# Linear attention and a gated linear unit on one core: output stored by one transfer a chunk instead of four, a head pair of q loaded by two instead of four

## The chip, the cores and the metric

The kernel runs on one core of a Trainium2 chip. The core has a matrix engine (TensorE, PE in the profile, with PEld for its weight loads), VectorE (DVE), ScalarE (ACT), GpSimd (POOL) and SyncE (SP), which computes nothing and issues transfers. Sixteen DMA engines move data between HBM and the core's memory, whichever queue issues the transfer. The metric is device time in microseconds of one execution.

## The reference

Two blocks follow each other. The first is linear attention with a norm for each head, the second a gated linear unit whose gate is a causal convolution over five tokens. There are 8 batches, 8 heads, 576 tokens, a head dimension of 64 (so 512 channels), all in float32; the weights arrive in float64.

```python
kv = einsum('bhsd,bhse->bhde', k, v)
out = einsum('bhsd,bhde->bhse', q, kv)
rms = sqrt(mean(out * out, axis=-1, keepdims=True) + 1e-06)
x = (out / rms * g_norm)            # then (B, H, S, D) -> (B, S, H*D)
gate = sigmoid(sum over k of conv_w[k] * x shifted by K-1-k tokens)
result = (gate * (x @ w_val)) @ w_out
```

## The kernel before

The whole order of the work is written out by hand in a list of some 1,200 steps (PLAN); each step is a function with its arguments, called in the list's order, and each engine and each queue runs its instructions in that order. Waits between them follow from the tiles that they read and write. Work of neighbouring batches is interleaved: while TensorE multiplies batch b by the weights, q, k and v of batches b + 1 and b + 2 are loaded, and the output of a pair of batches is stored later.

For a batch b the steps are:

- load_half (lines 302 to 311) loads half of k or v, 576 KB, in one transfer of 128 rows of two runs of 2,304 B. The k and v tiles of batches 2 to 7 have one buffer for each half, so the next load waits for kv_product.
- load_q (313 to 325) loads one pair of heads of q for batches 2 to 7. Batches 0 and 1 use load_q_rows (327) instead. Tokens stand in memory as token = t x 18 + n, with t from 0 to 31 and n from 0 to 17; a row t is one run of 18 x 64 values. The tile qs has room for three loads, so a load waits until the load three earlier has been transposed. It holds, for each of two heads r and for each half of the head dimension, 32 partitions t; the second half is read 32 values (128 B) further on, and each partition takes 1,120 values (4,480 B).
- turn_q (460) transposes 32 x 32 blocks on VectorE. Then kv_product (432) and raw_pair and raw_tail (via raw_product, 488) multiply on TensorE; square, sums, powers and normalise scale by the root.
- turn_blocks (595) transposes x on VectorE, and move_blocks (599) carries the blocks to their place by transfers within the core's memory, alternately on SP's and GpSimd's queue.
- gate_start, gate_tap, gate_end form the gate, val_fast (669) multiplies by w_val, gated multiplies the two.
- For a pair of batches i, fast_product (755) and out_product (707) multiply by w_out, and fast_keep (778) and keep_out (726) collect a chunk c of 128 rows in the tile ot, which has three buffers. Chunks 0 to 3 and 4 to 7 are the first 512 tokens of the two batches; chunk 8 holds the last 64 tokens of both.
- store (802) writes a chunk. The 128 partitions of ot are four blocks j of 32 tokens t; the output is viewed as rows_out[batch, n, t, channel], in which neighbouring t lie 18 x 512 values apart and neighbouring n 512 values. The last two chunks are stored by store_last (799), in two halves, one on SP's queue and one on ACT's.

All loads of q for batches 2 to 7 and nearly all stores go through SP's queue. SP takes eight completion counters in turn; a transfer waits until the one eight before it has landed.

Of the kernel before, what the change touches and what calls it, by code (L numbers as in the profile page):

```python
# [207 lines left out]
def kernel(  # L208
# [11 lines left out]
    nc = tc.nc  # L220
    B, H, S, D = q.shape
    C = H * D
    HP = H // 2
    NJ = S // P
    SF = NJ * P
    T = S - SF
    NK = C // P
    TB = 32
    NB = S // TB
# [3 lines left out]
    HB = P // TB  # L233
# [62 lines left out]
    st = {}  # L296

    def head(hp, r):

        return r * (H // 2) + hp  # L300
# [12 lines left out]
    def load_q(b, hp):  # L313
        t = qs[:, (b * HP + hp + 1) % 3]
        run = S // TB * D - TB
        flat = t.rearrange("p n d -> p (n d)")
        for half in range(2):
            for r in range(2):
                first = (2 * r + half) * TB
                nc.sync.dma_start(  # L320
                    out=flat[first:first + TB, 0:run],
                    in_=q[b, head(hp, r)].rearrange("(t n) d -> t (n d)", t=TB)[
                        :, half * TB:half * TB + run],
                )
        st["q", b, hp] = t

    def load_q_rows(b, r):
# [377 lines left out]
    rows_out = out.rearrange("b (t n) c -> b n t c", n=NB)  # L705
# [93 lines left out]
    def store_last(i, c, n):  # L799
        store(i, c, nc.scalar if n else nc.sync, range(n * HB // 2, (n + 1) * HB // 2))  # L800

    def store(i, c, queue=nc.sync, blocks=range(HB)):
        ot = st["ot", i, c]
        for j in blocks:
            bb, n = divmod(c * HB + j, NJ * HB) if c < 2 * NJ else (j // 2, NJ * HB + j % 2)
            queue.dma_start(out=rows_out[2 * i + bb, n], in_=ot[j * TB:(j + 1) * TB, :])

    steps = {f.__name__: f for f in (
        load_half, load_q, load_q_rows, stage_weight, narrow_weight, turn_cw, keep_cw, start_warm, warm_up,
        kv_product, kv_copy, turn_q, turn_q_rows, sort_q, raw_whole, raw_pair, raw_tail, square, sums, powers, normalise,  # L810
        turn_x, keep_x, turn_blocks, move_blocks, halo, gate_start, gate_tap, gate_end, val_product, keep_val, gated,
        val_sums, x_sums, val_fast, val_keep, out_product, keep_out, weight_sums, token_sums, fast_product, fast_keep,
        store, store_last)}
    with tc.manual_schedule():
        set_up()
# [33 lines left out]
```

## Time and profile before

| what | value |
|---|---|
| median of three runs | 306.25 us (304.12 to 307.25) |
| span of the profiled execution | 304.6 us |
| transfers issued by SP | 325 |
| HBM read, written | 39.21 MB, 9.44 MB |
| issue of one q load or one store on SP, median | 0.42 us each |
| transpose of one q tile on VectorE (two instructions) | 0.70 and 0.20 us |

All times below are from one profiled execution, whose span is 304.6 us; the runs' median is 1.65 us above it. In the profile a line such as L320 is a line of the kernel, SPq is SP's queue, and a group's row gives how many instructions it has, their busy time and the mean of one. The views in forty columns cut the span in equal slices of 7.6 us, each digit a tenth of busy time. The rows of the issue table give the size of one transfer and the median time from its issue to its landing. Of the kernel's time TensorE's matrix products are the largest part: the product with w_out (L774), with w_val (L682 and L633) and the attention products (L440, L501).

### The profile page before, as it was taken

The page shows a single profiled execution, that of the slowest core. Times are in us where ns is not written, and L with a number is a line of the kernel's source. Part 1 is how long each engine was busy: PE and PEld are TensorE (multiplying, and loading weights), DVE is VectorE, ACT ScalarE, POOL GpSimd, SP SyncE. Part 2 cuts the span into 40 slices and gives each one's busy share as a digit, 9 for nine tenths or more (in the row PEclk, how much of TensorE's full clock was granted, in tenths as well). Part 3 has the DMA queues.
Part 4 walks back from the last instruction along what each step waited for, and adds up shares of the span by engine and source line. Part 5 has one row for each costly group of instructions (what it writes and reads, how often), then busy time and mean ns, then how long its engine had stood idle before and what let it go on. Part 6 is the DMA issues. An engine that isn't in the chain of part 4 may idle for free.

```text
span 304.6 us, 8977 instructions
## 1 busy us (share of the span) xinstructions
PE 294.8 (97%) x3441; PEld 232.4 (76%) x3441; DVE 269.2 (88%) x474; ACT 193.7 (64%) x596; POOL 114.9 (38%) x127
## 2 busy tenths in 40 slices
PE   7899999999999999999999999999999999999993
PEld 7788778877787785777778757787878588888582
DVE  1169999999999999999999999999999999999612
ACT  1569989999768664884586547683787354535220
POOL 3027354406568217364338352345536631000000
PEclk9979999999999999999999999999999999999999
DMA  7999998088569756988689477927411621112423
GB/s 269 343 368 343 272 302 210 4 230 269 154 147 329 231 163 167 269 220 260 173 253 294 111 175 232 326 72 214 114 48 30 169 80 34 36 42 64 103 69 103
DMA packets 32074, 55.53 MB, mean 182 GB/s; under 512 B 6166, under 2 KB 14358, under 8 KB 32032
## 3 DMA queue, kind: packets, MB, share of 16 engines
q1 hardware_dynamic: 29520, 49.76, 55.7%
q0 software_dynamic: 1632, 3.17, 4.1%
q10 hardware_dynamic: 880, 2.03, 1.8%
q8 instruction: 27, 0.44, 0.6%
q14 instruction: 15, 0.12, 0.1%
HBM read 39.21 MB, written 9.44 MB: 160 GB/s over the span
## 4 chain that ended last, share of the span: by engine, by line
PE 89%; DVE 5%; DMA 2%; issue 1%; ACT 1%; DVEq 0%; ACTq 0%; SPq 0%
PE a L774 18%; PE cb L774 14%; PE va L682 13%; PE val L633 11%; PE vc L682 6%; PE kvps L440 6%; PE raw L501 5%; PE out L720 5%; PE vb L682 4%; PE qTps L477 4%; PE raw L512 2%; PE xTps L583 2%; DMA qs<-in_q_dram 2%; DVE gate L621 2%; DVE xs L667 1%
## 5 line engine op out<-in xcount | busy, mean ns | idle before, releaser
L552 POOL TENSOR_TENSOR rt<-ss,mhalf 128x8 f32<-128x8 f32 (+3 forms) x38 | 68.9, 1822 | 101.0 <-DVE ss L544 100.8
L621 DVE SCALAR_TENSOR_TENSOR gate<-xT,cwT,gate 128x576 f32<-128x576 f32 x128 | 101.8, 809 | 1.0
L571 ACT ACTIVATE x<-raw,rt 128x64 f32<-128x64 f32 x252 | 55.8, 351 | 7.2 <-POOL rt L552 4.2
L604 POOL DMA_DIRECT2D xT<-y x48 | 26.4, 557 | 25.5 <-DVE ot L784 14.0
L633 PE MATMUL val<-xT,wval 128*128 128x288 f32 x128 | 33.0, 411 | 0.0
L774 PE MATMUL a<-wsum,sums 128*128 128x256 f32 x128 | 32.4, 382 | 0.0
L628 ACT ACTIVATE gate<-gate 128x576 f32<-128x576 f32 x32 | 22.0, 692 | 11.7 <-DVE gate L621 11.4
L633 PEld LDWEIGHTS val<-xT,wval 128*128 128x128 f32 x128 | 23.5, 190 | 6.5 <-ACT xT L590 0.4
L544 DVE TENSOR_REDUCE ss<-sq 128x8 f32<-128x520 f32 (+1 forms) x40 | 24.7, 627 | 2.9 <-ACT sq L531 2.5
L774 PEld LDWEIGHTS a<-wsum,sums 128*128 128x128 f32 x128 | 24.0, 190 | 4.1 <-issue 0.6
L535 ACT ACTIVATE sq<-raw 128x256 f32<-128x256 f32 (+1 forms) x70 | 22.4, 403 | 7.3 <-PE raw L501 7.1
L682 PE MATMUL va<-xs,vsum 128*128 128x288 f32 x96 | 26.6, 409 | 0.0
L615 ACT ACTIVATE gate<-xT,cwT 128x576 f32<-128x576 f32 x32 | 25.2, 811 | 1.5 <-DVE gv L646 1.3
L646 DVE TENSOR_TENSOR gv<-gv,gate 128x576 f32<-128x576 f32 x32 | 23.6, 750 | 0.9 <-ACT gate L628 0.8
L682 PEld LDWEIGHTS va<-xs,vsum 128*128 128x128 f32 x96 | 18.0, 190 | 5.1 <-ACT x L571 0.4
L611 POOL COPY xT<-xT 128x124 f32<-128x124 f32 x32 | 17.5, 585 | 10.5 <-ACT xT L590 10.5
L501 PEld LDWEIGHTS raw<-kv,qT 64*64 64x64 f32 x1008 | 16.4, 134 | 5.3 <-issue 3.0
L440 PEld LDWEIGHTS kvps<-v,k 64*64 64x64 f32 x1008 | 15.9, 135 | 3.7 <-issue 1.9
L501 PE MATMUL raw<-kv,qT 64*64 64x64 f32 x1008 | 18.7, 221 | 0.0
L440 PE MATMUL kvps<-v,k 64*64 64x64 f32 x1008 | 17.6, 220 | 0.0
L774 PE MATMUL cb<-wsum,sums 128*128 128x256 f32 x64 | 16.9, 386 | 0.1
L774 PE MATMUL cb<-wout,gv 128*128 128x256 f32 x64 | 16.8, 385 | 0.0
(111 smaller groups left out, 542.3 us busy)
## 6 DMA issues: line engine op xcount, KB each, us to landing
qs<-in_q_dram SPq DMA_DIRECT2D x96, 140.0 KB, 4.2
out_dram<-ot SPq DMA_DIRECT2D x140, 64.0 KB, 1.7
k<-in_k_dram SPq DMA_DIRECT2D x14, 576.0 KB, 6.3
v<-in_v_dram SPq DMA_DIRECT2D x12, 576.0 KB, 6.5
xT<-y SPq DMA_DIRECT2D x48, 64.0 KB, 2.7
xT<-y POOLq DMA_DIRECT2D x48, 64.0 KB, 3.3
y<-in_moe_w_val_dram SPq DMA_DIRECT2D x4, 512.0 KB, 11.4
w_wout<-in_moe_w_out_dram SPq DMA_DIRECT2D x4, 512.0 KB, 6.3
```

What stands on the lines that cost most here:

```text
L440: nc.tensor.matmul(st["kvps", b][s][r * D:(r + 1) * D, i], st["k", b, i][rows, r, cols], st["v", b, i][rows, r, cols], start=(j == 0), sto ...
L501: nc.tensor.matmul(st["raw", b, c][r][cols, to * D:(to + 1) * D], st["qT", b][rows, hp, first:first + D], kvs[b % 2][rows, hp, :], start=T ...
L544: nc.vector.reduce_sum(out=st["ss", b][:, FIRST[c]:FIRST[c] + n], in_=st["sq", b, c][:, 0:n], axis=AX.X)
L552: nc.gpsimd.tensor_tensor(out=st["rt", b][:, which], in0=st["ss", b][:, which], in1=mhalf[:, which], op=ALU.pow)
L571: nc.scalar.activation(out=x[:, to * D:(to + 1) * D], in_=raw[:, h * D:(h + 1) * D], func=AF.Copy, scale=root[:, to:to + 1])
L604: (nc.sync if i % 2 else nc.gpsimd).dma_start(out=xTs[b % 2][i * TB:(i + 1) * TB, :, first:first + P], in_=y[a * TB:(a + 1) * TB, i])
L615: nc.scalar.activation(out=gate[:], in_=xTs[b % 2][:, jt, HALO:SX], func=AF.Copy, scale=cwT[:, K - 1, jt:jt + 1])
L621: nc.vector.scalar_tensor_tensor(out=gate[:], in0=xTs[b % 2][:, jt, tap * TB:tap * TB + S], scalar=cwT[:, tap, jt:jt + 1], in1=gate[:], op ...
L633: nc.tensor.matmul(val[:], wval[:, kc, jt * P:(jt + 1) * P], xTs[b % 2][:, kc, HALO + n * SV:HALO + (n + 1) * SV], start=(kc == 0), stop=( ...
L646: nc.vector.tensor_tensor(out=both, in0=both, in1=st["gate", b, jt][:], op=ALU.mult)
L682: nc.tensor.matmul(st[bank, "val", b, mj][:], weights_[:, k], tokens()[:, k], start=(n in (0, 1, 3) and k == 0), stop=(k == NK // 2 - 1), ...
L774: nc.tensor.matmul(st[bank, i, p], tokens()[:, k], weights_[:, k], start=(n < 2 and k == 0), stop=(k == NK // 2 - 1), skip_group_check=True)
```

## The change

store writes a chunk by one transfer: the four blocks of the output are four neighbouring n, so the output side is four blocks of 32 rows and the tile's side 128 rows. Chunk 8 is stored by two transfers, one for each batch, and a half of store_last by one. load_q loads one head of the pair by one transfer: the memory side is two halves, 32 values apart and overlapping, of 32 rows, the tile's side 64 partitions. The bytes, the tiles and the order of the steps stay.

```diff
@@ load_q
         run = S // TB * D - TB
-        flat = t.rearrange("p n d -> p (n d)")
-        for half in range(2):
-            for r in range(2):
-                first = (2 * r + half) * TB
-                nc.sync.dma_start(
-                    out=flat[first:first + TB, 0:run],
-                    in_=q[b, head(hp, r)].rearrange("(t n) d -> t (n d)", t=TB)[
-                        :, half * TB:half * TB + run],
-                )
+        for r in range(2):
+            begin = q[b, head(hp, r)]
+            nc.sync.dma_start(
+                out=t.rearrange("p n d -> p (n d)")[2 * r * TB:2 * (r + 1) * TB, 0:run],
+                in_=bass.AP(begin.tensor, begin.offset, [[TB, 2], [S // TB * D, TB], [1, run]]))
@@ store
-        ot = st["ot", i, c]
-        for j in blocks:
-            bb, n = divmod(c * HB + j, NJ * HB) if c < 2 * NJ else (j // 2, NJ * HB + j % 2)
-            queue.dma_start(out=rows_out[2 * i + bb, n], in_=ot[j * TB:(j + 1) * TB, :])
+        ot, first, m = st["ot", i, c], blocks[0], len(blocks)
+        if c < 2 * NJ:
+            bb, n = divmod(c * HB, NJ * HB)
+            queue.dma_start(
+                out=rows_out[2 * i + bb, n + first:n + first + m], in_=ot[first * TB:(first + m) * TB, :])
+            return
+        for bb in range(2):
+            queue.dma_start(out=rows_out[2 * i + bb, NJ * HB:NB], in_=ot[bb * T:(bb + 1) * T, :])
```

## The prediction

> **What bounds the kernel now.** First the busy times and the chain of waits, to find the engine that sets the end.
>
> ```profile
> PE 294.8 (97%) x3441; PEld 232.4 (76%) x3441; DVE 269.2 (88%) x474; ACT 193.7 (64%) x596; POOL 114.9 (38%) x127
> ...
> PE 89%; DVE 5%; DMA 2%; issue 1%; ACT 1%; DVEq 0%; ACTq 0%; SPq 0%
> ```
>
> TensorE is busy for 294.8 of 304.6 us, and only 2% of the chain is a transfer. The transfers are hidden, so cheaper issuing can bring almost nothing; what matters is whether they stay hidden. So the DMA part is read next.
>
> ```profile
> DMA  7999998088569756988689477927411621112423
> GB/s 269 343 368 343 272 302 210 4 230 269 154 147 329 231 163 167 269 220 260 173 253 294 111 175 232 326 72 214 114 48 30 169 80 34 36 42 64 103 69 103
> DMA packets 32074, 55.53 MB, mean 182 GB/s; under 512 B 6166, under 2 KB 14358, under 8 KB 32032
> ## 3 DMA queue, kind: packets, MB, share of 16 engines
> q1 hardware_dynamic: 29520, 49.76, 55.7%
> ```
>
> For the first 70% of the span the 16 DMA engines are 70 to 90% busy together: there is no great reserve. Two rates per engine come from here: the slice of 368 GB/s has the engines nearly full, 368 / 16 = 23.0 GB/s each; over the whole queue, 49.76 MB in 0.557 x 16 x 304.6 us is 18.3 GB/s per busy engine. The packets tell how a transfer is dealt. By the shapes in the program the SP queue's 325 transfers have 24,320 rows, one packet each; 29,520 - 24,320 = 5,200 = 325 x 16. Every transfer closes with 16 small packets, one per engine: each is spread over all 16.
>
> ```profile
> qs<-in_q_dram SPq DMA_DIRECT2D x96, 140.0 KB, 4.2
> out_dram<-ot SPq DMA_DIRECT2D x140, 64.0 KB, 1.7
> k<-in_k_dram SPq DMA_DIRECT2D x14, 576.0 KB, 6.3
> v<-in_v_dram SPq DMA_DIRECT2D x12, 576.0 KB, 6.5
> xT<-y SPq DMA_DIRECT2D x48, 64.0 KB, 2.7
> ```
>
> Last, the SP queue in order of time gives the stretch in which q is loaded (lines 320), and the chain where the last of it is used.
>
> ```profile
> 28.31 1.74 SPq L320 DMA_DIRECT2D qs<-in_q_dram  x4
> ...
> 205.84 1.77 SPq L320 DMA_DIRECT2D qs<-in_q_dram  x4
> ...
> 244.90 57.24 SPq L806 DMA_DIRECT2D out_dram<-ot  x52
> ```
>
> ```profile
> 215.57 1.09 PE raw L501 x64
> ```
>
> All 96 loads go out between 28.3 and 207.6 us, and the product that uses the last of them (raw_pair 7 3) starts at 215.6; behind it lie 304.6 - 215.6 = 89.0 us of nearly unbroken TensorE.
>
> **The change, part by part.** No compute instruction moves on any engine, and the order on SP stays. Issues: 96 q loads become 48, 140 + 4 stores become 40 + 2. At 0.42 us each (1.74 us for four) that frees (48 + 100) x 0.42 = 62 us of SP, which computes nothing; in the middle its gain is nothing, under TensorE. At the end it may save two issues, 0.8 us. The eight completion counters that SP's transfers take in turn are reused later too; worth nothing on the path.
>
> What is new is the shape. Before, both sides of every transfer begin with the same count of rows, 32 or 128 on this queue. Now a q load reads [2, 32, 1120] into [64, 1120], and a store writes [4, 32, 512] from [128, 512] (chunk 8 and the last two chunks [2, 32, 512] from [64, 512]). No row of this trace has such a transfer, so its price is bounded from both sides. One end: dealt over 16 engines as now, it costs what the same bytes cost before. Other end: an engine's share must be one piece on both sides, and if pieces are cut along the outermost dimension, the sides share only 2 pieces for q and 4 (or 2) for stores; then two engines carry all of q. I take the second end: all 325 transfers cut alike on both sides along their outermost rows, and a finer share of the new ones would need a cut inside the second dimension of one side, which nothing here shows. [...]
>
> The sum for the fullest engine, from the first load_q to the last, in the program's own order: 48 q loads x 143,360 B = 6.88 MB; 24 loads of k and v x 36,864 B = 0.88 MB; 3 of w_out x 32,768 B = 0.10; 64 block moves x 4,096 B = 0.26; 13 stores x 65,536 B = 0.85; 4 of the half-chunk kind x 65,536 B = 0.26. Together 9.24 MB; spread over 16, the same transfers were 37.6 / 16 = 2.35 MB an engine. At 23.0 GB/s that is 402 us, in place of the 179 us between the two timeline rows; q alone takes 299 us. So q cannot stay hidden. Everything on the SP queue falls in behind: on the two full engines k, v, the odd block moves and the stores wait for the q issued ahead of them, so kv_product, val_fast and raw_pair all start late, and TensorE waits for DMA.
>
> Does the fullest engine run without a break? A load_q waits for the transpose (turn_q, DVE) of the load three earlier, so up to six transfers, 6 x 143,360 B / 23.0 = 37 us, are queued ahead. SP also halts at stores (in the waits of its queue, 43.3 us in 12 waits for VectorE's last additions, at most 9.0 us each); 37 us covers these, so I add nothing.
>
> After the last q lands: about 1 us until its completion is seen and 0.9 us for turn_q's two transposes (0.70 and 0.20 us in the timeline), then the 89.0 us. Stores in that stretch: 65,536 B on the fullest engine, 2.9 us a chunk, against one chunk per 57.24 / 13 = 4.4 us: hidden, until the last two chunks. These are issued from 299.4 us on:
>
> ```profile
> 299.44 1.83 ACTq L806 DMA_DIRECT2D out_dram<-ot  x4
> 299.53 0.42 DVE L797 COPY ot<-a 128x256 f32<-128x256 f32 x1 [0.17 <-PE a L774]
> ```
>
> Now 5.2 us lead from there to the end. Four half-chunk stores on two engines leave 4 x 65,536 B = 262 KB on each, 11.4 us, plus 3 us of landing (1.7) and of closing after it: 14.4, so 9 more.
>
> Sum: 28.3 + 402 + 2 + 89 + 9 = 530 us of span. The median of the runs shown, 306.25, lies 1.65 above this execution's span; predicted 532 us. With 25 GB/s per engine (the load stretch from 20 to 27 us reaches 400 GB/s) the 402 become 370 and the time 500; with 18.3 they become 505 and the time 635.
>
> **Rivals.** (a) Dealt over 16 as before: the change does nothing but save issues. For it: 16 closing packets per transfer, whatever its shape, in 325 cases. Against it: no case had unlike sides. TensorE has 9.8 us idle in all, 6 at the start and 5 at the end, and only the end's 0.8 us is touched: 305 us, no slower. It decides if the dealing counts rows and not outer dimensions. [...]
>
> (b) The two engines hinder each other. Engine 0 would write partitions 0 to 31 of a tile's half and engine 1 partitions 32 to 63, in step. In the packet records of this trace a row of 2,048 B, stored out of 32 partitions, takes 84 ns in many cases and about 148 in nearly as many; a q row of 4,480 B takes 173 at best, 246 at the median and 300 at the upper quartile. So something shared slows rows up to 1.75 times. At 300 ns a row q takes 48 x 32 x 0.300 = 461 us, and the other 2.36 MB at 18.3 GB/s 129 us: 590 in place of 402, 720 us in all. It decides if a q row's median in the new trace is near 300 ns and not 173 to 195. [...]
>
> (c) q stays spread and only the stores, cut in four, are narrow: 30 x 65,536 B over the whole span is little for engines that had room, and the end pays 9 us: 315 us.
>
> **How the numbers follow.** Two or four engines at 18 to 25 GB/s: 0.70 (500 to 635, likeliest 532). (b) 0.16. (c) 0.05. (a) 0.09. The range takes the first case, with some room below it for a rate a little over 25 GB/s, and half of (b): 475 to 720. Faster or slower is told from no change at 1%, some 3 us. Only (a) can be no slower, and a gain of 3 us needs more than the end holds: faster 0.03, same 0.06, slower 0.91.
>
> **What would show it.** The SP queue's packets: 24,320 rows with 48 x 2 + 30 x 4 + 10 x 2 + 89 x 16 = 1,660 closing packets, 25,980 in all, if it is dealt over 2 and 4; 27,152 under (a). The DMA share falls to a few tenths in the first two thirds while TensorE shows gaps; the chain turns to DMA qs<-in_q_dram; q loads land after 8 us and more (143,360 B / 23.0 GB/s = 6.2 us of rows, with others ahead) in place of 4.2. After the last raw_pair about 89 us follow, as now. Wrong would be a landing of about 4 us, or TensorE gaps that VectorE or SP's halts end.

## The result, and the profile after

The changed kernel takes 554.2 us (median of six runs, 551.29 to 555.78) against 305.41 us for the kernel before (304.12 to 307.25), a ratio of 1.816 with a 95% interval of 1.811 to 1.822. Predicted were 532 us, between 475 and 720. The profiled execution has a span of 549.5 us. These are its busy times, its forty slices, its packets and its chain of waits, from the page:

```profile
span 549.5 us, 8754 instructions
...
PE 339.6 (62%) x3441; PEld 261.5 (48%) x3441; DVE 273.0 (50%) x474; ACT 193.6 (35%) x596; POOL 112.0 (20%) x127
...
PE   7997568153795525852529562495405988798770
...
PEclk9998778776798566875859977696857899799986
DMA  9935222352531223331123522333312204011111
...
q1 hardware_dynamic: 25980, 49.75, 28.0%
...
DMA 56%; PE 15%; SPq 13%; DVE 7%; ACT 3%; issue 2%; POOL 1%; ACTq 0%; DVEq 0%
DMA qs<-in_q_dram 32%; DMA out_dram<-ot 22%; SPq L318 8%; PE a L770 5%; PE cb L770 3%; PE va L678 2%; DVE gate L617 2%; SPq L807 2%; DMA v<-in_v_dram 1%; SPq L310 1%; POOL rt L548 1%; PE raw L497 1%; DVE qT L459 1%; PE vc L678 1%; SPq L803 1%
```

The same 49.75 MB go over SP's queue, but with 25,980 packets: 24,320 rows and 1,660 closing packets, where there were 5,200. That is the count of 48 loads on two engines, 30 stores on four and 10 on two, to the packet. The DMA engines are busy for two or three tenths in the middle, and still the transfers are what is waited for. That fits a few full engines beside idle ones; the records do not name the engines, and the runs below decide it. TensorE has gaps in nearly every slice. The chain, 2% transfers before, is now 56% transfers: q first, then the stores.

The waits by engine name both (waiting engine and line, what it waits for, us in all, times, longest):

```profile
DVE qT L459 <- DMA qs<-in_q_dram: 160.5, 17, 21.9
...
ACT ot L782 <- DMA out_dram<-ot: 49.0, 10, 11.5
ACT ot L784 <- DMA out_dram<-ot: 45.8, 10, 22.6
...
PEld kvps L436 <- DMA k<-in_k_dram: 36.2, 4, 11.8
```

VectorE waits 160 us in front of the transposes of q; before, none of VectorE's transposes had waited for its load at all. In the chain a load of q lies for 19 to 28 us from issue to landing. ScalarE waits 95 us for an ot tile that its store still holds; of these, 33.5 us lie behind 427.4 us, after the last q, and the others in the stretch with q. k, whose loads are among the 89 transfers with 16 closing packets, is waited for as well, 36.2 us in 4 times; that its shares on the full engines stand behind q is a reading of these waits, not shown by itself.

### The profile page after: what moved, and what is told of

It reads as the page before. It is cut to its first block, busy times and chain, and to the rows that moved or that the text cites. A ratio compares the mean times of both kernels' runs of the same rounds, so it can differ in the third digit from the quotient of the medians.

```text
span 549.5 us, 8754 instructions
## 1 busy us (share of the span) xinstructions
PE 339.6 (62%) x3441; PEld 261.5 (48%) x3441; DVE 273.0 (50%) x474; ACT 193.6 (35%) x596; POOL 112.0 (20%) x127
## 3 DMA queue, kind: packets, MB, share of 16 engines
q1 hardware_dynamic: 25980, 49.75, 28.0%
## 4 chain that ended last, share of the span: by engine, by line
DMA 56%; PE 15%; SPq 13%; DVE 7%; ACT 3%; issue 2%; POOL 1%; ACTq 0%; DVEq 0%
DMA qs<-in_q_dram 32%; DMA out_dram<-ot 22%; SPq L318 8%; PE a L770 5%; PE cb L770 3%; PE va L678 2%; DVE gate L617 2%; SPq L807 2%; DMA v<-in_v_dram 1%; SPq L310 1%; POOL rt L548 1%; PE raw L497 1%; DVE qT L459 1%; PE vc L678 1%; SPq L803 1%
## 5 line engine op out<-in xcount | busy, mean ns | idle before, releaser
L459 DVE STREAM_TRANSPOSE qT<-qs 128x512 f32<-128x512 f32 x24 | 17.0, 708 | 160.5 <-DMA qs<-in_q_dram 160.5
L770 PE MATMUL a<-wsum,sums 128*128 128x256 f32 x128 | 42.5, 471 | 43.0 <-ACT ot L782 20.2
L497 PE MATMUL raw<-kv,qT 64*64 64x64 f32 x1008 | 25.0, 256 | 54.2 <-DVE qT L459 54.2
L436 PE MATMUL kvps<-v,k 64*64 64x64 f32 x1008 | 25.9, 276 | 48.8 <-DMA k<-in_k_dram 34.5
L770 PEld LDWEIGHTS a<-wsum,sums 128*128 128x128 f32 x128 | 29.7, 240 | 52.0 <-ACT ot L782 22.7
L497 PEld LDWEIGHTS raw<-kv,qT 64*64 64x64 f32 x1008 | 21.6, 165 | 61.0 <-DVE qT L459 55.1
L436 PEld LDWEIGHTS kvps<-v,k 64*64 64x64 f32 x1008 | 23.7, 185 | 53.7 <-DMA k<-in_k_dram 36.2
L770 PE MATMUL cb<-wout,gv 128*128 128x256 f32 x64 | 20.7, 453 | 24.8 <-ACT ot L784 24.8
L624 ACT ACTIVATE gate<-gate 128x576 f32<-128x576 f32 x32 | 22.1, 699 | 36.3 <-DVE gate L617 36.2
L770 PEld LDWEIGHTS cb<-wout,gv 128*128 128x128 f32 x64 | 13.8, 224 | 28.5 <-ACT ot L784 26.2
L780 DVE TENSOR_TENSOR ot<-a,ot 128x256 f32<-128x256 f32 x16 | 6.7, 417 | 38.8 <-ACT ot L784 27.9
```

Source lines behind the costliest of these rows:

```text
L436: nc.tensor.matmul(st["kvps", b][s][r * D:(r + 1) * D, i], st["k", b, i][rows, r, cols], st["v", b, i][rows, r, cols], start=(j == 0), sto ...
L497: nc.tensor.matmul(st["raw", b, c][r][cols, to * D:(to + 1) * D], st["qT", b][rows, hp, first:first + D], kvs[b % 2][rows, hp, :], start=T ...
L770: nc.tensor.matmul(st[bank, i, p], tokens()[:, k], weights_[:, k], start=(n < 2 and k == 0), stop=(k == NK // 2 - 1), skip_group_check=True)
```

## The experiments

All times are medians; each ratio is to runs of the kernel before on the same chip. Theory A: a transfer is dealt over as many engines as the outermost counts of its two sides share, and always over the same ones (the expectations say the first; the records name no engine). The rivals B to E are those of the expectations, not the prediction's (a) to (c). What the prediction, the expectations and this text call the last raw_pair is raw_pair 7 3, the first product that needs the last load of q; raw_pair 7 1 and raw_tail 7 still follow it.

**Each half of the change alone.** The first run has the new store and the old load_q, the second the new load_q and the old store (the two halves of the diff above).

> Stores of the changed kernel, q loads of the kernel before. Theory A (a transfer is dealt over as many engines as the outermost counts of both sides share, 4 or 2 here, always the first ones): until the last q load the fullest engine has about 3.2 MB in 180 us, so that stretch stays near 215 us to the last raw_pair; behind it the stores hold the three ot tiles as in the changed kernel, some 122 us in place of 89. Time 340 us (320 to 350), SP queue 24,320 rows plus 30 x 4 + 10 x 2 + 185 x 16 = 3,100 closing packets, 27,420 in all. Rival C (the long end of the changed kernel is TensorE's lower clock after the q stalls, not the stores): about 315 us, the last raw_pair to the end near 95 us.

Measured: 349.8 us, ratio 1.147 (1.143 to 1.151), 27,420 packets. The last raw_pair starts at 226.3 us, 11 later than before, and 120.5 us follow it in place of 89.1.

> q loads of the changed kernel, stores of the kernel before. Theory A: the stretch from the first load_q to the landing of the last loses the stores' 0.86 MB on the fullest engine, 37 us at 23 GB/s: 395 - 37 = 358 us. Behind the last raw_pair 89 to 93 us as before. Time about 482 us (460 to 500). Rival C (the clock makes the end long): 120 us behind the last raw_pair, time above 505 us.

Measured: 499.9 us, ratio 1.641 (1.635 to 1.648), at the upper edge of the range. From the first row of q to the last it is 375 us, 17 more than expected, and behind the last raw_pair 89.9 us. So q lengthens the part in front of the last raw_pair and the stores mainly the part behind it, and rival C falls: after 375 us of gaps, with a clock of 0.78 on average, the end runs as before. The two halves cost 45 and 195 us, together nearly the 249 of both.

**The same count and size of transfers, another outermost dimension.** In load_q the memory side names the 32 tokens first:

```diff
-                in_=bass.AP(begin.tensor, begin.offset, [[TB, 2], [S // TB * D, TB], [1, run]]))
+                in_=bass.AP(begin.tensor, begin.offset, [[S // TB * D, TB], [TB, 2], [1, run]]))
```

> Two q loads a head pair, as in the changed kernel, with sides as unlike as there (memory side [32, 2, 1120], tile side [64, 1120]), but the 32 tokens outermost on the memory side; stores of the kernel before. Tokens and halves land in other partitions than the reference's order asks for, with the same bytes, tiles and instructions. Theory A: 16 engines share it, q lands in some 4 to 6 us, time 305 us (302 to 309), SP queue 24,320 + 277 x 16 = 28,752 packets. Rival B (unlike sides, or fewer and larger transfers, are slow in themselves): as slow as q loads of the changed kernel alone, over 400 us.

Measured: 306.0 us, ratio 1.003 (1.000 to 1.007), a span of 306.7 us. The second run does the same to the stores as well (the two of chunk 8 likewise):

```diff
-                out=rows_out[2 * i + bb, n + first:n + first + m], in_=...
+                out=rows_out[2 * i + bb, n + first:n + first + m].rearrange("n t c -> t n c"), in_=...
```

> Both parts of the change with the 32 tokens outermost on the memory side: q as in the run before, and one store a chunk with memory side [32, 4, 512] and tile side [128, 512]. q and the output land in another order of rows than the reference's; same bytes and transfer counts as the changed kernel. Theory A: 16 engines for all, time 304 us (300 to 308), a gain of at most 1 us over the kernel before at the end; SP queue 24,320 + 177 x 16 = 27,152 packets. Rival B: over 400 us.

Measured: 305.0 us, ratio 1.002 (0.999 to 1.004). From the packet table of each and, for the second, the row of its stores among the issues:

```profile
q1 hardware_dynamic: 28752, 49.76, 57.8%
```

```profile
q1 hardware_dynamic: 27152, 49.75, 55.3%
...
out_dram<-ot SPq DMA_DIRECT2D x30, 256.0 KB, 2.5
```

These two runs decide the case. Sides of different shapes cost nothing here (306.0 us); fewer and larger transfers cost nothing (305.0 us); the same 48 loads and 30 stores with 32 in front instead of 2 and 4 bring the 249 us back. They also show what joining transfers is worth here when it is dealt well: nothing that can be measured (ratios 1.003 and 1.002), so no version that beats the kernel before follows from it. (Both runs put q, and the second the output too, in another order of rows than the reference's. With the reference's order, q's halves and the output's blocks stand in blocks of 32 partitions, and the tokens can't simply be named first on both sides.)

**How the time follows the number of engines.** q in loads of 64 rows with an outermost count of 4 or 8, by overlapping reads, so that the tile holds other tokens than the reference asks for:

```diff
-                in_=bass.AP(begin.tensor, begin.offset, [[TB, 2], [S // TB * D, TB], [1, run]]))
+                in_=bass.AP(begin.tensor, begin.offset, [[5 * S // TB * D, 4], [S // TB * D, 2 * TB // 4], [1, run]]))
```

> Two q loads a head pair of 64 rows as in the changed kernel, but with memory side [4, 16, 1120] (a head's tokens read from other, overlapping places, so the q tile holds other tokens; same bytes and instructions); stores of the kernel before. Theory A with the measured rate of the run with q alone (8.38 MB in 375 us, 22.3 GB/s): dealt over 4 engines the fullest has 3.44 + 1.50 = 4.94 MB, 221 us from the first load to the landing of the last, then some 94 us: 345 us (325 to 365); SP queue 24,320 + 48 x 4 + 229 x 16 = 28,176 packets. Rival B (the two engines' meeting at the same memory places costs, not their number): about the 306 us of 16 engines or the 500 us of two.

Measured: 380.2 us, ratio 1.244 (1.238 to 1.251): outside the range expected, though the packets are the 28,176 forecast and the time lies between that of 16 engines and of two. Either the engines ran dry now and then, or rows took longer. The next run gave q five tiles, three before (`% 5` in place of `% 3` in load_q, and the tile to match):

> The run with q dealt over 4 engines (380 us against a forecast of 345), with five q tiles in place of three, so that a load waits for the transpose of the load five earlier. Theory E (the 34 us more were breaks: with three tiles the engines run dry now and then): 345 to 360 us. Theory A3 (the four engines are full all the time and rows take longer than assumed: 4,480 B rows 219 ns on average, 673 us over 4 engines, and all other rows 1,495 us over 16, together 261 us for the 254 between the first load and the landing of the last): within 8 us of 380.

Measured: 380.2 us, ratio 1.243 (1.236 to 1.251). Deeper prefetch brings nothing here (380.2 us with three tiles and with five), as theory A3 expects of full engines. For 8 engines the factor is 3 and the counts 8 and 8:

> As the run with 4 engines, with memory side [8, 8, 1120], so 8 engines (the q tile holds other tokens). Theory A: the fullest engine has 48 x 35,840 B = 1.72 MB of q and 1.50 MB of the rest; at the 19.4 GB/s of the run with 4 engines 166 us, just under the 182 us that TensorE needs for this stretch: 306 to 318 us; SP queue 24,320 + 48 x 8 + 229 x 16 = 28,368 packets.

Measured: 328.5 us, ratio 1.077 (1.072 to 1.083), again above what was expected, with the 28,368 packets forecast. SP's queue in these two runs, 4 engines and 8:

```profile
q1 hardware_dynamic: 28176, 49.76, 45.4%
```

```profile
q1 hardware_dynamic: 28368, 49.76, 54.8%
```

Why both were higher shows when the durations of all rows between the first and the last of q are added up from the packet records, q's over the engines it has, the stores' over theirs, and the rest over 16:

| q over | stores over | mean q row, ns | rows on the fullest engine, us | first to last q row, us |
|---|---|---|---|---|
| 16 (kernel before) | 16 | 255 | 134 | 180 |
| 16 (two loads a pair) | 16 | 284 | 142 | 182 |
| 8 | 16 | 276 | 200 | 205 |
| 4 | 16 | 219 | 265 | 254 |
| 2 | 16 | 193 | 386 | 375 |
| 2 (changed kernel) | 4 | 187 | 415 | 395 |

(The sums for two and four engines pass the stretch by 11 to 20 us. Rows on one engine seem to overlap a little, since those of q reach 2.1 times the length of a stretch on two engines; whether this is all of it is not shown.) In these six runs the stretch is, to within 20 us, the longer of the 180 us of the kernel before, where TensorE sets it, and the rows on the fullest engine. The expectations for 4 and 8 used the rate of the run with two engines and with four; a row of q took longer with four and eight engines (219 and 276 ns) than with two (193), which eats part of what spreading gains. Why a row takes longer was not tried.

**How the stores lengthen the end.** Two transfers of [2, 32, 512] a chunk, so two engines in place of four:

```diff
+            for h in range(first, first + m, 2):
+                queue.dma_start(out=rows_out[2 * i + bb, n + h:n + h + 2], in_=ot[h * TB:(h + 2) * TB, :])
```

> q loads of the kernel before; each chunk stored by two transfers of [2, 32, 512], so on two engines with 131,072 B each in place of four with 65,536 B. Theory A: a store lands some 2.7 us later (32 more rows of 84 ns), which the three ot tiles pass on to each of about 19 chunks behind the last raw_pair: that part 120 + 50 = 170 us, the time 350 + 50 and up to 15 more before it: 410 us (385 to 440). Rival C (clock): about 355 us.

Measured: 415.5 us, ratio 1.365 (1.358 to 1.372); 157 us behind the last raw_pair and 255 before it. The total is as expected, but shared out otherwise: 13 us less than expected in the end, and 14 us more in front than the 226 + 15 that were allowed; that the two nearly cancel is luck. Then the stores on four engines again, with more room for what waits to be stored (the two other places that name the tile likewise):

```diff
-            st["ot", i, 2 * p + row] = work.tile([P, C], FP32, tag="ot", bufs=3, name=f"ot{i}_{2 * p + row}")
+            st["ot", i, 2 * p + row] = work.tile([P, C], FP32, tag="ot", bufs=6, name=f"ot{i}_{2 * p + row}")
```

> Stores of the changed kernel, q loads of the kernel before, and six ot tiles in place of three. Theory A2 (the end is long because a store holds one of only three tiles some 6 us in place of under 2): with six the part behind the last raw_pair falls from 120 to some 95 us, the time from 350 to 315 to 325 us. Rival D (the first four engines are full in that part): no change, 345 to 350 us.

Measured: 329.1 us, ratio 1.078 (1.074 to 1.083), 103 us behind the last raw_pair: both above what theory A2 expected (315 to 325, and some 95). The waits for ot in the run with three tiles, and the last copy into an ot tile with six (timeline of VectorE):

```profile
ACT ot L788 <- DMA out_dram<-ot: 23.3, 9, 5.5
...
ACT ot L786 <- DMA out_dram<-ot: 15.8, 6, 5.3
```

```profile
307.40 0.42 DVE L797 COPY ot<-a 128x256 f32<-128x256 f32 x1 [0.17 <-PE a L774]
```

With six tiles these waits are gone, and from the last raw_pair (222.1) to this copy's end (307.8) it is 85.7 us, as in the kernel before (215.5 to 299.95, 84.5); with three tiles it is 105.4. What is left of the excess lies behind the copy: 17.5 us until the last stores have landed, against 4.7 in the kernel before and 15.1 with three tiles. So theory A2 holds for the part in front of the copy and rival D falls there; the draining at the end stays, and theory A2 had left it out.

**Are they always the same two engines?** The new load_q issued on GpSimd's queue:

```diff
-            nc.sync.dma_start(
+            nc.gpsimd.dma_start(
```

> q loads as in the changed kernel but issued on GpSimd's queue; stores of the kernel before. Theory A (dealt over two engines by the outermost counts) leaves open which two: if the two change from load to load, every engine has about 2.4 MB again and q lands in some 8 us each, several at once: 306 to 345 us. If they are the same two: 480 to 520 us as with q alone on SP.

Measured: 375.2 us, ratio 1.228 (1.222 to 1.235): neither of the two. The profiled execution took 379.3 us. The packet records tell more than the time. With the loads on SP, the durations of q rows in a stretch of 10 us add up to at most 2.1 times its length, however many loads are queued. If each load had a pair of its own, queued loads would run side by side; so this speaks for one pair throughout. On GpSimd's queue they reach 6.6 times the length in a stretch of 20 us, so several pairs work at once. The end of the changed kernel shows the same for ACT's queue: from 538 to 546 us SP and ACT store half-chunks at once, two engines each, and the rows add up to only 1.07 times the time on SP's queue and 1.02 on ACT's, 2.1 together. That speaks for one pair that both queues share. The records do not name the engines, so which two they are is not shown. Why this run is not faster stays open: q rows take 322 ns there on average, each load comes with 464 packets of 4 B (the queue has 23,088 of them, 816 in the kernel before), and the loads stand in GpSimd's order behind its powers.

## Why the prediction was right, and where it was off

| step of the sum | predicted, us | measured, us |
|---|---|---|
| until the first q load (predicted: its issue; measured: its first row) | 28.3 | 26.8 |
| first q row to last | 402 | 395.0 |
| to the last raw_pair | 2 | 5.6 |
| last raw_pair to the last copy into ot | 84.5 | 106.6 |
| from there to the end | 13.7 | 15.5 |
| span | 530 | 549.5 |

The mechanism is the one predicted: dealing over two and four engines fits the packets to the last one, and the runs that only reorder the memory side show that it is the cause. That the same two engines carry every load of q, and that the stores fall to these two as well, is a term of the sum that no run shows, since the records name no engine; what the runs showed in its place is that rows of q on SP's queue add up to at most 2.1 times the length of a stretch, and that the new stores lengthen the stretch with q from 375 to 395 us. The main term, the fullest engine's 9.24 MB at 23.0 GB/s, came out at 395 us, 23.4 GB/s. That SP's halts are covered by the queue of loads held too, as far as it was tried: with four engines, five q tiles in place of three changed nothing. Two readings were loose and carry no weight in the sum: of the 28 slices that it calls 70 to 90% busy eight stand at 6 tenths or below, and of TensorE's idle time 2.1 us lie in the first 7.6 us, not 6.

The term that was off is the stores behind the last q; the sign "about 89 us follow" failed with it, 122 us did. The prediction set 2.9 us of rows a chunk against 4.4 us between chunks and called them hidden until the last two. It counted the engine's time and not the time that a store holds its tile. The chain of the changed kernel shows it (start, length, what):

```profile
484.04 5.88 DMA out_dram<-ot
489.94 0.04 ACTq L784
489.98 0.04 issue
490.02 0.37 ACT ot L784
490.39 0.68 ACT gate L611
...
492.62 5.91 DMA out_dram<-ot
498.55 0.04 ACTq L784
498.58 0.04 issue
498.62 0.37 ACT ot L784
```

From the end of the copy or addition that completes a chunk to the landing of its store, with what is queued ahead of it, is 5.9 us; in this part of the kernel before, a chunk's four transfers took 3.1 us at the median from the first issue to the last landing. Then a ScalarE copy takes the freed tile at once, and TensorE's next product waits for the copy that frees its bank (in the whole run 31.5 us in 8 waits for the copies of L784, 20.2 in 6 for those of L782). The stretch is 106.6 - 84.5 = 22 us longer, more than the 19.5 us by which the span passes the forecast; the shorter stretch with q takes some of it back. That three tiles are the reason was shown with the new stores alone (105.4 us, and 85.7 with six); with both halves of the change it was not tried. The 5.6 us up to the last raw_pair, in place of 2, have the same cause: TensorE's product ahead of it waits 6.5 us for a ScalarE copy, which had waited 9.0 us for a store. The wait for ot was in the trace of before already, 9.8 us in all behind its last raw_pair where the changed kernel has 38.7, so the tiles had no room to spare:

```profile
ACT ot L728 <- DMA out_dram<-ot: 4.2, 1, 4.2
DVE ot L784 <- DMA out_dram<-ot: 4.1, 1, 4.1
...
ACT ot L788 <- DMA out_dram<-ot: 0.8, 1, 0.8
...
ACT ot L786 <- DMA out_dram<-ot: 0.7, 1, 0.7
```

The prediction also held the issues to be cheaper, 62 us of SP freed. Instead an issue of q took 2.5 us at the median and up to 12.6, where it had been 0.42, and all issues of q and of stores on SP 213 us in place of 100. Size alone does not do it: the same 280 KB over 16 engines were issued in 0.59 us at the median and 1.3 at most. That SP stands in the issue because its engines still have work queued is a reading that the trace does not prove. Line 318 alone is 8% of the chain.

Rival (a), dealing over 16, and (c), only the stores narrow, fall with the packets. The price of (c) was off as well: it is the run with the new store alone, which took 349.8 us and not 315, since here too a store's hold on its tile was left out. Rival (b), two engines that hinder each other, falls as well: a q row takes 173 ns at the median, a store row 84, among the best durations of the trace before (173 ns or less for a quarter of its q rows, 84 or less for half of its store rows). Whether the two ever wrote partitions 32 apart at the same moment, the records do not show.

## What to carry to other kernels

When transfers are joined, look at the outermost count of both sides of the new one, not at its size: the q loads that were [32, ...] and became [2, 32, ...] were dealt over two engines here, and with them alone the time went from 305.0 to 499.9 us. On SP's queue the closing packets told in these runs over how many engines transfers were dealt (25,980 packets in place of 29,520), before any time is read; where the order of rows is free, put the large count in front on both sides (here 32 on the memory side, 64 or 128 on the tile's: 305.0 us). Where a transfer becomes slower, ask how long it holds its buffer (here 5.9 us, against 3.1 before), and not only how long the engine works on it (2.9 us by the prediction's 23.0 GB/s).

## What the runs showed of the hardware that was not expected

TensorE's clock. In the changed kernel the granted clock falls to one half in 22 pieces of 3.4 to 20.5 us; in the 3.4 us before each of them TensorE was busy for less than half of the time (0 to 0.49). Over the stretch with q it is 0.77 on average, and TensorE's busy time grows from 294.8 to 339.6 us for the same products. The lengths of the pieces, all but the last, which runs to the end of the record, are whole multiples of 3.41 us; what sets this length is not shown. The lower clock does not lengthen the end: in the run with q alone the part behind the last raw_pair is 89.9 us, as before (89.1). In the stretch with q TensorE waits for transfers, so it should hardly count there either, though no run separates the two.

Rows of q were faster where fewer engines carried them. A row of 4,480 B takes 173 ns at the median with two engines, 174 with four, 249 with eight, 222 to 288 with sixteen; the mean goes from 187 ns with two to between 250 and 284 with sixteen.
